# Decode attention with a gated feed-forward on one core: order of the last weight loads, a two-strip result, and x on another queue

## The chip, the core and the metric

The kernel runs on one core of a Trainium2 chip. A core has five engines that run side by side and wait for each other through semaphores: TensorE (PE, matrix products, into PSUM), VectorE (DVE), ScalarE (ACT), GpSimd (POOL) and SyncE (SP, which here only issues transfers). Transfers run on 16 DMA engines; each engine's instruction stream can issue them on a queue of its own. The metric is the time of one execution on the device in microseconds, lower is better.

## What is computed

One decode step of a block with attention and a gated feed-forward in parallel, for batch B = 4, one token, width D = 640:

```python
x = A_x                                   # (4, 1, 640)
xn = layernorm(x)
q = (xn @ wq)                             # 32 heads of 192
k, v = last 2048 rows of the caches       # W = max(256, 8192 // 4)
p = softmax(q k^T * 192**-0.5)
attn = (p v) @ wo                         # (32*192) x 640
ffn = (silu(xn @ w1) * (xn @ w3)) @ w2    # 640 -> 1536 -> 640
return x + attn + ffn                     # bf16
```

All inputs are bf16. Keys and values of 32 heads, four sequences and 2048 rows are 201 MB, and nearly all of the traffic.

## The kernel before, in words

**Tiling.** A head's keys for all four sequences are one tile `kt` of 128 partitions (32 groups of rows by 4 sequences) by 64 rows by 192 elements, 3072 KB; its values are a tile `vt` of the same size. Each is one transfer (`load_k` L97, `load_v` L102). Three buffers each for keys and values. The scores are made on VectorE: per chunk of 16 rows a product with the broadcast q (`mult`, L205), summed in parts by TensorE with an identity (`adder`, L215) and finished by VectorE (`reduce_tile`, L224). Per head follows the softmax (`chain_lmax` to `chain_bc`, exponentials on ScalarE at L256, `rowsum`), then the product with the values on TensorE (`pv`, L275, 32 matmuls into `o_ps`), a copy by ScalarE (L279), and `fold` (L288, L292). Four heads make a group: `ge_tr` (L298 to L300) transposes the group's outputs to `oT` (128 x 6 x 4), and `ge_proj` (L309) multiplies them with the group's output weights into `acc`, two strips of 4 rows by 320 columns at partitions 0 and 32, accumulated over all eight groups.

**Order.** The program order is written out as slots: head h has the four slots 4h to 4h+3, and `add(slot, phase, fn, ...)` puts a piece of work in a slot. The slots end at 128 (`end`), with `pv` nine slots (`L`) behind `mult`. All transfers are issued by SyncE in this order and wait there for their buffer. At the end the order of issues is: key tile 31 and the output weights of the last group (slot 116), value tiles 29 (slot 117), 30 (slot 121) and 31 (slot 125), w1 and w3 (slot 126), and w2 in three parts (slot 128). w1, w3 and w2 take the three key buffers.

**Feed-forward.** `ffn_mm(1)` (slot 138) makes the gate: 15 matmuls into `gt` (L329), a copy (L333) and Silu (L336) on ScalarE, the latter with a load of its function table ahead of it. `ffn_mm(3)` (slot 139) makes the up part with 15 matmuls, a copy (L333) and the product on VectorE (L340). `ffn_transpose` (L346, L347) turns the product into `hT` (128 x 4 x 96). Then 24 matmuls (L406) with w2 give `ff`, again two strips of 4 rows.

**Result.** `acc` is copied strip by strip side by side into a 4 x 640 tile (L397), x is added (L399), the two strips of `ff` are copied by ScalarE (L409) and VectorE (L410), the two are added (L412), and SyncE issues one transfer of the result (L413).

**Start.** SyncE issues x (L113), three transfers of wq into the value buffers (L120) and three key tiles (L99). GpSimd makes the identities and fills the three z tiles (L137). VectorE and ScalarE make the layernorm (L143 to L160), TensorE the q products (L187).

Of the kernel before, what the change touches and what calls it, by code (L numbers as in the profile page):

```python
# [11 lines left out]
BF16 = mybir.dt.bfloat16  # L12
ALU = mybir.AluOpType
# [5 lines left out]
def kernel(  # L19
# [26 lines left out]
    nc = tc.nc  # L46
    P = 128
    B, Sq, D = A_x.shape
    _, H, Sk, Dh = A_k_cache.shape
# [5 lines left out]
    NC = NJ // CH  # L55
# [5 lines left out]
    RPP = (HG * Dh) // P  # L61
# [4 lines left out]
    DH = D // 2  # L66
# [9 lines left out]
    const = ctx.enter_context(tc.tile_pool(name="const", bufs=1))  # L76
# [3 lines left out]
    ppool = ctx.enter_context(tc.tile_pool(name="pr", bufs=PBUFS))  # L80
    qpool = ctx.enter_context(tc.tile_pool(name="qbc", bufs=2))
    opool = ctx.enter_context(tc.tile_pool(name="o", bufs=2))
    small = ctx.enter_context(tc.tile_pool(name="small", bufs=3))
# [3 lines left out]
    ps_acc = ctx.enter_context(tc.tile_pool(name="ps_acc", bufs=1, space=MemoryType.PSUM))  # L87

    kts, vts, prs, pss, scs, zts = {}, {}, {}, {}, {}, {}
    qbcs, wos, o_pss, rss, rcps, o_sbs, o_bfs, ges, chs = ({} for _ in range(9))  # L90
    mult_insts = {}
    ORDER_DEP = mybir.DependencyInfo(mybir.DependencyClass.NoSync, mybir.DependencyReason.SCHED_ONLY)

# [16 lines left out]
        wos[hg] = wt  # L110

    x_sb = const.tile([B, D], BF16, name="x_sb")
    nc.sync.dma_start(out=x_sb[:], in_=A_x.rearrange("b s d -> (b s) d"))  # L113
    RV = NJ * Dh // (H * Dh)
    wq_rows = A_wq.rearrange("(p kc) n -> p kc n", kc=KC)
    wqs = []
# [18 lines left out]
    for i in range(NZ):  # L135
        z = const.tile([P, NJ // 2, 32], BF16, name=f"z{i}")
        nc.gpsimd.memset(z[:], 0.0)  # L137
        zs.append(z)
    rowsel = const.tile([P, 2 * B], FP32, name="rowsel")
    nc.vector.tensor_reduce(out=rowsel[:], in_=idf[:].rearrange("p (g c) -> p c g", g=NG)[:, 0:2 * B, :], axis=AX.X, op=ALU.add)  # L140

# [34 lines left out]
    acc = ps_acc.tile([64, DH], FP32, name="acc")  # L176

    q_pss = []
    for k in range(NB):
        pool, tag = ((ps_add, "ps"), (ps_o, "o_ps"))[k // 2]  # L180
        qp = pool.tile([P, QW], FP32, tag=tag)
        q_pss.append(qp)
    for kc in range(KC):
        for k in range(NB):
            for g in range(NG):
                off = (k * NG + g) * QW
                nc.tensor.matmul(q_pss[k][32 * g:32 * g + 32, :], lhsT=xnT[:, kc, :],  # L187
                                 rhs=wqs[kc // RV][:, kc % RV, off:off + QW], start=(kc == 0), stop=(kc == KC - 1))
# [105 lines left out]
    def ge_tr(hg):  # L294
        gp = ps_t.tile([P, RPP, B], BF16, tag="t")
        of = o_bfs.pop(hg)[:].rearrange("r h d -> r (h d)")
        for i in range(RPP):
            nc.tensor.transpose(out=gp[:, i, :], in_=of[:, i:OW:RPP], identity=idb[0:B, 0:B])  # L298
        oT = small.tile([P, RPP, B], BF16, tag="oT", bufs=2)
        nc.vector.tensor_copy(out=oT[:], in_=gp[:])  # L300
        ges[hg] = oT

    def ge_proj(hg, i):
        oT = ges[hg]
        wo_t = wos[hg]
        st = (hg == 0 and i == 0)
        sp = (hg == H // HG - 1 and i == RPP - 1)
        for t in range(2):
            nc.tensor.matmul(acc[32 * t:32 * t + B, :], lhsT=oT[:, i, :], rhs=wo_t[:, i * D + t * DH:i * D + (t + 1) * DH],  # L309
                             start=st, stop=sp)  # L310

    ffn = {}
# [38 lines left out]
    def add(slot, phase, fn, *args):  # L351
        sched[slot].append((phase, len(sched[slot]), fn, args))

    for h in range(H):
# [4 lines left out]
        for c in range(NC):  # L359
            s = s0 + c  # L360
# [12 lines left out]
        add(max(qg * QP * NC - 3, -1), 6, q_bcast, qg)  # L373
    for hg in range(H // HG):
        a = (hg + 1) * HG * NC - 1 + L
        add(hg * HG * NC + 4, 0, wo_load, hg)
        add(a + 2, 6, ge_tr, hg)
        for i in range(RPP):
            add(a + 3, 6, ge_proj, hg, i)
    hT = const.tile([P, CF, 32 * NF], BF16, name="hT")  # L380

    end = H * NC
    add(end - 2, 0, ffn_load, 1)
    add(end - 2, 0, ffn_load, 3)
    for n in range(NF):
        add(end, 0, w2_load, n)
    add(end + L + 1, 7, ffn_mm, 1)
    add(end + L + 2, 7, ffn_mm, 3)
    add(end + L + 3, 7, ffn_transpose)

    for s in sorted(sched):
        for phase, _, fn, args in sorted(sched[s], key=lambda e: (e[0], e[1])):
            fn(*args)

    attn_bf = ppool.tile([B, D], BF16, tag="pr")
    for t in range(2):
        nc.vector.tensor_copy(out=attn_bf[:, t * DH:(t + 1) * DH], in_=acc[32 * t:32 * t + B, :])  # L397
    t1 = ppool.tile([B, D], BF16, tag="pr")
    nc.vector.tensor_tensor(out=t1[:], in0=x_sb[:], in1=attn_bf[:], op=ALU.add)  # L399

    ff = ps_o.tile([64, DH], FP32, tag="o_ps")
    w2t = ffn[2]
    for n in range(NF):
        for c in range(CF):
            for t in range(2):
                nc.tensor.matmul(ff[32 * t:32 * t + B, :], lhsT=hT[:, c, 32 * n:32 * n + B], rhs=w2t[:, n, c, t * DH:(t + 1) * DH],  # L406
                                 start=(n == 0 and c == 0), stop=(n == NF - 1 and c == CF - 1))
    ffn_bf = ppool.tile([B, D], BF16, tag="pr")
    nc.scalar.copy(out=ffn_bf[:, 0:DH], in_=ff[0:B, :])  # L409
    nc.vector.tensor_copy(out=ffn_bf[:, DH:D], in_=ff[32:32 + B, :])  # L410
    res = ppool.tile([B, D], BF16, tag="pr")
    nc.vector.tensor_tensor(out=res[:], in0=t1[:], in1=ffn_bf[:], op=ALU.add)  # L412
    nc.sync.dma_start(out=out.rearrange("b s d -> (b s) d"), in_=res[:])  # L413


# [28 lines left out]
```

## Time and profile before

| what | value |
|---|---|
| median of 3 runs | 530.42 us (529.5 to 531.95) |
| profiled execution, its own time | 530.08 us |
| profiled execution, span from first to last instruction | 528.3 us |
| HBM read | 222.96 MB, 422 GB/s over the span |
| busy share of TensorE, VectorE, ScalarE, GpSimd | 68%, 64%, 15%, 1% |
| mean granted TensorE clock | 0.848 |
| value tile of head 30, issue to landing | 468.12 us, 34.2 us |
| value tile of head 31, issue to landing | 483.36 us, 26.31 us |
| w1, issue to landing | 483.95 us, 30.3 us |
| w3, issue to landing | 485.1 us, 33.7 us |
| w2 in three parts, first issue; to landing | 494.47 us; 25.8 to 27.0 us |
| table load for Silu | 1.28 us |

The span is what the profile sees of an execution; its own time is 1.78 us longer. A landing is the moment at which the last bytes of a transfer are there. In the profile a line such as `L329 PE MATMUL gt<-wt,xnT` names the source line, the engine, the operation, and the written and read tiles; the granted clock is a share of the full clock of TensorE. In the chain of waits each row is a start, a duration and what the end was waiting for then.

### The profile page before, as it was taken

To read this page: it belongs to the slowest core of one execution; us is meant where nothing else is said; L and a number is where in the kernel's file an instruction comes from. 1 tells how busy PE (TensorE), PEld (TensorE's weight loads), DVE (VectorE), ACT (ScalarE), POOL (GpSimd) and SP (SyncE) were. 2 spreads that over 40 slices of the span, in tenths; PEclk is the share of its full clock that TensorE was granted. 3 is DMA by queue.
4 is the path that set the end of the run, shared out by engine and by line. 5 is a ranking of instruction groups with operands and counts; after the bars stand their busy time and mean duration, and the time that the engine had idled before them with its cause. 6 is when DMAs were issued, how large, how long until landed. Compare 5 with 4: busy or idle time off the path is not lost.

```text
span 528.3 us, 5868 instructions
## 1 busy us (share of the span) xinstructions
PE 360.4 (68%) x2384; PEld 149.5 (28%) x2384; DVE 340.3 (64%) x477; ACT 76.8 (15%) x319; POOL 3.8 (1%) x11
## 2 busy tenths in 40 slices
PE   1456767877577777777566976767587775667765
PEld 1122222332222322223222322223232322223323
DVE  4069766677666657776566677766567776666702
ACT  2101111101111111011111110111111011111112
POOL 2000000000000000000000000000000000000000
PEclk9999988788777887878888787888878878788858
DMA  8999999999999999999999999999999999999994
GB/s 350 424 437 430 432 432 435 427 425 439 432 431 430 429 437 430 434 433 432 428 434 430 429 432 432 430 435 432 426 437 426 433 433 430 431 432 431 432 423 176
DMA packets 11562, 223.33 MB, mean 423 GB/s; under 512 B 1288, under 2 KB 1296, under 8 KB 2704
## 3 DMA queue, kind: packets, MB, share of 16 engines
q1 hardware_dynamic: 11536, 222.97, 98.4%
q8 instruction: 18, 0.29, 0.2%
q14 instruction: 8, 0.07, 0.0%
HBM read 222.96 MB, written 0.01 MB: 422 GB/s over the span
## 4 chain that ended last, share of the span: by engine, by line
DMA 59%; DVE 20%; PE 16%; ACT 3%; issue 1%; SPq 0%; DVEq 0%; ACTq 0%
DMA kt<-in_A_k_cache_dram 54%; DVE pr L205 14%; PE ps L215 10%; DMA vt<-in_A_v_cache_dram 5%; DVE sc L224 4%; PE o_ps L275 3%; ACT z L256 2%; PE acc L309 1%; ACT o_sb L279 1%; PE gt L329 0%; PE gp L298 0%; PE ff L406 0%; PE fp L288 0%; DVE lmax L231 0%; PE tb L262 0%
## 5 line engine op out<-in xcount | busy, mean ns | idle before, releaser
L215 PE MATMUL ps<-pr,idb 128*128 128x512 bf16 x768 | 239.5, 468 | 111.8 <-DVE sc L224 103.3
L205 DVE TENSOR_TENSOR pr<-kt,qbc 128x3072 bf16<-128x3072 bf16 x128 | 223.3, 1746 | 36.7 <-DMA kt<-in_A_k_cache_dram 36.5
L215 PEld LDWEIGHTS <-idb 128*128 128x128 bf16 x768 | 85.1, 114 | 240.3 <-issue 190.6
L224 DVE TENSOR_REDUCE sc<-ps 128x16 f32<-128x512 f32 x128 | 87.0, 680 | 0.6 <-PE ps L215 0.6
L275 PE MATMUL o_ps<-vt,z 128*32 128x384 bf16 x1024 | 56.7, 340 | 3.3 <-DMA vt<-in_A_v_cache_dram 3.3
L256 ACT ACTIVATE z<-sc,negm 128x64 bf16<-128x64 f32 x128 | 45.7, 423 | 89.7 <-DVE negm L252 89.7
L279 ACT COPY o_sb<-o_ps 128x384 f32<-128x384 f32 x32 | 15.1, 472 | 297.9 <-PE o_ps L275 297.9
L252 DVE TENSOR_TENSOR negm<-mt,mbias 128x4 f32<-128x4 f32 x32 | 5.2, 161 | 70.4 <-PE mt L250 70.4
L292 DVE TENSOR_SCALAR o_bf<-fp,rcp 4x192 bf16<-4x192 f32 x32 | 12.9, 405 | 56.1 <-PE fp L288 28.4
L288 PE MATMUL fp<-o_sb,rowsel 128*4 128x192 f32 x128 | 27.3, 338 | 14.6 <-ACT o_sb L279 14.6
L275 PEld LDWEIGHTS <-z 128*32 128x32 bf16 x1024 | 25.7, 98 | 28.5 <-issue 17.5
L256 ACT ACTIVATION_READ_ACCUMULATOR z<-sc,negm 128x1 f32 x128 | 23.9, 187 | 0.0
L288 PEld LDWEIGHTS fp<-o_sb,rowsel 128*4 128x4 f32 x128 | 8.6, 87 | 26.3 <-ACT o_sb L279 21.0
L262 PE MATMUL tb<-ones_f,rs 128*4 128x1 f32 x64 | 6.2, 166 | 12.9 <-ACT z L256 12.9
L250 PE MATMUL mt<-nsc,gmq 1*128 1x4 f32 x64 | 12.2, 258 | 1.3 <-DVE gmq L244 1.3
L250 PEld LDWEIGHTS mt<-nsc,gmq 1*128 1x128 f32 x64 | 9.4, 183 | 12.4 <-issue 10.4
L187 PE MATMUL qp<-wt,xnT 128*32 128x384 bf16 x80 | 7.0, 522 | 6.4 <-DMA wt<-in_A_wq_dram 6.4
L309 PE MATMUL acc<-wt,oT 128*4 128x320 bf16 x96 | 10.6, 307 | 0.6 <-DVE oT L300 0.5
L262 PEld LDWEIGHTS tb<-ones_f,rs 128*4 128x4 f32 x64 | 3.7, 86 | 23.6 <-ACT z L256 22.0
L236 PE MATMUL mt<-idf,lmax 128*1 128x128 f32 x32 | 9.7, 304 | 0.7 <-DVE lmax L231 0.4
L264 DVE RECIPROCAL rcp<-tb 4x1 f32<-4x1 f32 x32 | 4.9, 152 | 8.2 <-PE tb L262 8.2
L199 ACT CAST qbc<-bp 128x384 bf16<-128x384 f32 x16 | 7.6, 485 | 7.7 <-PE bp L196 7.7
(61 smaller groups left out, 81.4 us busy)
## 6 DMA issues: line engine op xcount, KB each, us to landing
kt<-in_A_k_cache_dram SPq DMA_DIRECT2D x32, 3072.0 KB, 36.6
vt<-in_A_v_cache_dram SPq DMA_DIRECT2D x32, 3072.0 KB, 40.3
wt<-in_A_wo_dram SPq DMA_DIRECT2D x8, 960.0 KB, 36.6
wt<-in_A_wq_dram SPq DMA_DIRECT2D x2, 3072.0 KB, 17.0
wt<-in_B_w_dram SPq DMA_DIRECT2D x2, 1920.0 KB, 32.0
w2t<-in_B_w_dram SPq DMA_DIRECT2D x3, 640.0 KB, 26.4
wt<-in_A_wq_dram SPq DMA_DIRECT2D x1, 1536.0 KB, 20.2
x_sb<-in_A_x_dram SPq DMA_DIRECT2D x1, 5.0 KB
```

The lines of the kernel that those rows point to most:

```text
L205: mi = nc.vector.tensor_tensor(out=pr[:], in0=kts[h][:, c * CH:(c + 1) * CH, :], in1=qbcs[h // QP][:, h % QP, :].unsqueeze(1).to_broadcast ...
L215: nc.tensor.matmul(ps[:], lhsT=idb[:], rhs=pr[:, :, kk * DD:(kk + 1) * DD], start=(kk == 0), stop=(kk == NK - 1))
L224: ri = nc.vector.tensor_reduce(out=scs[h][:, c * CH:(c + 1) * CH], in_=pss.pop(s)[:], axis=AX.X, op=ALU.add)
L236: nc.tensor.transpose(out=mt[0:1, 0:P], in_=chs[h][0][:], identity=idf[:])
L250: nc.tensor.matmul(mt[:, P:P + B], lhsT=gmq[:].rearrange("o q b -> o (q b)"), rhs=nsc[:], start=True, stop=True)
L256: nc.scalar.activation(out=z[:, :, 0:2, b], in_=sc[:].rearrange("p (j s) -> p j s", s=2), func=ACTF.Exp, bias=negm[:, b:b + 1], scale=SCAL ...
L262: nc.tensor.matmul(tb[:], lhsT=rss.pop(h)[:], rhs=ones_f[:], start=True, stop=True)
L275: nc.tensor.matmul(o_ps[32 * g:32 * g + 32, :], lhsT=z[:, jj, :], rhs=vt[:, 2 * jj:2 * jj + 2, :], start=(jj < NG), stop=(jj >= NJ // 2 - NG))
L279: nc.scalar.copy(out=o_sb[:].rearrange("r two d -> r (two d)"), in_=o_pss.pop(h)[:])
L288: nc.tensor.matmul(fp[:], lhsT=rowsel[:, two * B:(two + 1) * B], rhs=o_sb[:, two, :], start=(two == 0), stop=(two == 1))
L292: nc.vector.tensor_scalar_mul(out=o_bfs[hg][:, hl, :], in0=fp[:], scalar1=rcps.pop(h)[:, 0:1])
L309: nc.tensor.matmul(acc[32 * t:32 * t + B, :], lhsT=oT[:, i, :], rhs=wo_t[:, i * D + t * DH:i * D + (t + 1) * DH], start=st, stop=sp)
```

## The change

Five edits:

- **Loads.** w1 is issued in slot 124, ahead of value tile 31 (slot 125); the output weights of the last group move from slot 116 to slot 126, behind that tile; w3 goes to slot 127; w2 stays in slot 128.
- **Gate.** `ffn_mm(1)` moves from slot 138 to slot 133, phase 0, which is ahead of the value matmuls of head 31; `ffn_mm(3)` takes slot 138. On TensorE the order is then: value matmuls of head 30, gate, fold of head 30, value matmuls and fold of head 31, transposes, projection, up, transposes, w2. On ScalarE the gate's copy, the table load and Silu stand ahead of head 31's copy.
- **32-column weights.** `oT` becomes two fixed tiles of 32 columns per step, filled with zeros once by GpSimd, of which 4 columns are written per group; the projection and the w2 matmuls use 32 columns, so that all 64 rows of `acc` and `ff` are written.
- **Result.** The two strips stay where they are: one copy of `acc` (64 x 320), one add of `x_st`, and one add that reads `ff` from PSUM; two transfers of the result, one on SyncE's queue and one on ScalarE's.
- **x.** x is loaded on ScalarE's queue, followed there by two small transfers into the two strips of `x_st`, which GpSimd fills with zeros first.

```diff
-    nc.sync.dma_start(out=x_sb[:], in_=A_x.rearrange("b s d -> (b s) d"))
+    x_rows = A_x.rearrange("b s d -> (b s) d")
+    nc.scalar.dma_start(out=x_sb[:], in_=x_rows)
+    x_st = const.tile([64, DH], BF16, name="x_st")
+    nc.gpsimd.memset(x_st[:], 0.0)
+    for t in range(2):
+        nc.scalar.dma_start(out=x_st[32 * t:32 * t + B, :], in_=x_rows[:, t * DH:(t + 1) * DH])
...
+    oTs = []
+    for i in range(2):
+        oT = const.tile([P, RPP, 32], BF16, name=f"oT{i}")
+        nc.gpsimd.memset(oT[:], 0.0)
+        oTs.append(oT)
...
-        oT = small.tile([P, RPP, B], BF16, tag="oT", bufs=2)
-        nc.vector.tensor_copy(out=oT[:], in_=gp[:])
-        ges[hg] = oT
+        nc.vector.tensor_copy(out=oTs[hg % 2][:, :, 0:B], in_=gp[:])
...
-            nc.tensor.matmul(acc[32 * t:32 * t + B, :], lhsT=oT[:, i, :], rhs=wo_t[:, i * D + t * DH:i * D + (t + 1) * DH],
+            nc.tensor.matmul(acc[32 * t:32 * t + 32, :], lhsT=oT[:, i, :], rhs=wo_t[:, i * D + t * DH:i * D + (t + 1) * DH],
                              start=st, stop=sp)
...
-        add(hg * HG * NC + 4, 0, wo_load, hg)
+        add(hg * HG * NC + (4 if hg < H // HG - 1 else 14), 0, wo_load, hg)
...
     end = H * NC
-    add(end - 2, 0, ffn_load, 1)
-    add(end - 2, 0, ffn_load, 3)
+    add(end - 4, 0, ffn_load, 1)
+    add(end - 1, 0, ffn_load, 3)
     for n in range(NF):
         add(end, 0, w2_load, n)
-    add(end + L + 1, 7, ffn_mm, 1)
-    add(end + L + 2, 7, ffn_mm, 3)
+    add(end + L - NC, 0, ffn_mm, 1)
+    add(end + L + 1, 7, ffn_mm, 3)
     add(end + L + 3, 7, ffn_transpose)
...
-    attn_bf = ppool.tile([B, D], BF16, tag="pr")
-    for t in range(2):
-        nc.vector.tensor_copy(out=attn_bf[:, t * DH:(t + 1) * DH], in_=acc[32 * t:32 * t + B, :])
-    t1 = ppool.tile([B, D], BF16, tag="pr")
-    nc.vector.tensor_tensor(out=t1[:], in0=x_sb[:], in1=attn_bf[:], op=ALU.add)
+    attn_bf = ppool.tile([64, DH], BF16, tag="pr")
+    nc.vector.tensor_copy(out=attn_bf[:], in_=acc[:])
+    t1 = ppool.tile([64, DH], BF16, tag="pr")
+    nc.vector.tensor_tensor(out=t1[:], in0=x_st[:], in1=attn_bf[:], op=ALU.add)
...
-                nc.tensor.matmul(ff[32 * t:32 * t + B, :], lhsT=hT[:, c, 32 * n:32 * n + B], rhs=w2t[:, n, c, t * DH:(t + 1) * DH],
+                nc.tensor.matmul(ff[32 * t:32 * t + 32, :], lhsT=hT[:, c, 32 * n:32 * n + 32], rhs=w2t[:, n, c, t * DH:(t + 1) * DH],
                                  start=(n == 0 and c == 0), stop=(n == NF - 1 and c == CF - 1))
-    ffn_bf = ppool.tile([B, D], BF16, tag="pr")
-    nc.scalar.copy(out=ffn_bf[:, 0:DH], in_=ff[0:B, :])
-    nc.vector.tensor_copy(out=ffn_bf[:, DH:D], in_=ff[32:32 + B, :])
-    res = ppool.tile([B, D], BF16, tag="pr")
-    nc.vector.tensor_tensor(out=res[:], in0=t1[:], in1=ffn_bf[:], op=ALU.add)
-    nc.sync.dma_start(out=out.rearrange("b s d -> (b s) d"), in_=res[:])
+    res = ppool.tile([64, DH], BF16, tag="pr")
+    nc.vector.tensor_tensor(out=res[:], in0=ff[:], in1=t1[:], op=ALU.add)
+    out_rows = out.rearrange("b s d -> (b s) d")
+    nc.sync.dma_start(out=out_rows[:, 0:DH], in_=res[0:B])
+    nc.scalar.dma_start(out=out_rows[:, DH:D], in_=res[32:32 + B])
```

More of the change, by code (lines that the diff above doesn't have):

```diff
@@ L89 @@
     kts, vts, prs, pss, scs, zts = {}, {}, {}, {}, {}, {}
-    qbcs, wos, o_pss, rss, rcps, o_sbs, o_bfs, ges, chs = ({} for _ in range(9))
+    qbcs, wos, o_pss, rss, rcps, o_sbs, o_bfs, chs = ({} for _ in range(8))
     mult_insts = {}
@@ L298, in ge_tr @@
             nc.tensor.transpose(out=gp[:, i, :], in_=of[:, i:OW:RPP], identity=idb[0:B, 0:B])
-        oT = small.tile([P, RPP, B], BF16, tag="oT", bufs=2)
-        nc.vector.tensor_copy(out=oT[:], in_=gp[:])
-        ges[hg] = oT
+        nc.vector.tensor_copy(out=oTs[hg % 2][:, :, 0:B], in_=gp[:])
     def ge_proj(hg, i):
-        oT = ges[hg]
+        oT = oTs[hg % 2]
         wo_t = wos[hg]
```

## The prediction

> **What bounds the kernel now.** I read the page first (span, slices, queue rows), then the chain of waits over the last 20 us, then the timeline and the issue rows of the end and of the start, then the stretches in which the granted TensorE clock changed. The slices show one resource that is full:
>
> ```profile
> span 528.3 us, 5868 instructions
> ...
> PEclk9999988788777887878888787888878878788858
> DMA  8999999999999999999999999999999999999994
> ...
> q1 hardware_dynamic: 11536, 222.97, 98.4%
> ```
>
> The transfer engines are busy from the first slice to the last; no other engine is. So the time is three pieces: what passes before the stream starts, the stream of 223 MB, and what follows its last bytes. The change moves no byte out of the stream, so it can touch only the ends. The end, in the chain of waits:
>
> ```profile
> 483.36 26.31 DMA vt<-in_A_v_cache_dram
> ...
> 516.44 2.27 PE gt L329 x10
> 518.72 0.02 issue
> 518.74 0.58 ACT t_bf L333
> 519.32 0.02 issue
> 519.34 1.28 ACT L336
> 520.62 0.01 issue
> 520.63 0.63 ACT sg L336
> 521.26 0.48 ACT t_bf L333
> ...
> 523.05 1.84 PE ff L406 x24
> 524.89 0.02 issue
> 524.91 0.49 DVE ffn_bf L410
> ...
> 525.50 0.48 DVE res L412
> ```
>
> The last value tile (head 31) lands at 483.36 + 26.31 = 509.67. Behind it come the attention output, the gate matmuls, then on ScalarE copy, table load (1.28 us), Silu and a second copy, one after the other; then product, transposes, 24 output matmuls, copy, add. The result is ready at 525.98, and 2.32 us later the span ends. Beside that chain the stream itself runs on: w3, issued at 485.1, takes 33.7 us and lands at 518.8, and by the stretches of 0.15 us the last w2 packets move until about 522.9. The chain starts its w2 matmuls at 523.05, so the two are only 0.1 us apart there.
>
> **The change, part by part.**
>
> *Order of transfers.* w1 (1920 KB) goes ahead of the head-31 value tile, and the last output-weight group (960 KB) from ahead of it to behind it; the sum up to w3 stays. A 3072 KB value tile took 7.31 us (502.36 to 509.67), so 960 KB is 2.28 us and 1920 KB 4.57 us. Head 30's value tile lands at 500.08 instead of 502.36, w1 at 504.65 (before about 514.25), head 31's at 511.95, 2.28 us later than before; the output weights at 514.2; w3 and w2 where they were. SyncE's waits don't starve the stream: w1 takes the buffer of key tile 29, whose products ended before 465, so it issues right behind value tile 30 (468.1); value tile 31 still issues near 483.4, w3 behind it, w2 at 494.5, each over 23 us ahead of its landing.
>
> *Gate matmuls.* They now stand on TensorE ahead of head 31's value matmuls; behind the wait for w1 stand the fold of head 30 and then head 31, and nobody needs those before 511.5. Cover: 504.65 to 511.95. At half clock the gate takes 2.5 us (13 took 2.45 us there), then copy 0.58, table 1.28, Silu 0.63, all over by 510. This takes 1.28 + 0.63 us of ScalarE out of the end; what is late next is w3, at 518.8. Head 31's own chain (2.75 value matmuls, 0.60 copy, 1.46 fold, 0.48, 0.47, 0.23, then 12 projection matmuls, about 1.7 at half clock) ends at 519.6 at half clock and near 516.9 at full clock, so w3 is the later one wherever the clock is full.
>
> *x on ScalarE's queue.* The first wq issue moves from 1.15 to 0.73, as x's issue (0.35 us, start 0.73) leaves SyncE: 0.42 us for the whole stream, if first bytes follow issue. Bounds: 0 (if the engines weren't ready) to 0.42; I take 0.42, because the issue rows are back to back and wq's bytes start within 0.9 us of the issue. What x now shares with wq: even 4 us late it is hidden, since the first product waited for the first key tile at 30.41 while q was ready at 25.24. ScalarE's three issues (about 1.1 us) and the wait for the small fill on GpSimd stand ahead of the table load, and that is used first at 6.28. The third key tile's issue waits for x's landing; 1.5 us of wait against some 18 us of wq queued. Cost nothing. GpSimd's three new fills (at most 0.9 us each, as the z fills) lie behind z, used after 45, and the identity is late by some 0.2 us of slack.
>
> *32 columns instead of 4.* The same matmul count and moved columns; the weight loads of 32 columns took 98 ns (z) and those of 4 columns 86 or 87 ns, and overlap. From -0.1 to +0.3 us over 24 matmuls; I take 0.
>
> *The result.* Out: copy 0.49 + add 0.48 with gaps, 524.89 to 525.98 = 1.09 us. In: one add of 64x320 from PSUM; nearest rows are the 4x320 cast from PSUM (0.49) and the 4x640 add (0.48): bounds 0.3 to 0.6, I take 0.49 + 0.03. One copy and the add with x lie under the transposes and the w2 matmuls, as their two copies did. Two output transfers of 2.5 KB on two queues replace one of 5 KB: 2.32 us from result to end, bounds 2.1 to 2.7; I keep 2.32.
>
> *Sum*, all 0.42 earlier: w3 518.38; up matmuls 1.36 at full clock (row at 518.82) 519.74; copy 0.60 520.34; product 0.46 520.80; transposes 0.42 521.22; copy 0.40 521.62; 24 w2 matmuls 1.88 523.50 (the last eight start at 522.9, the stream ends at 522.5: no wait); add 0.52 524.02. Before: 525.98. Gain 1.96 us (0.42 start, 0.57 result, the rest the ScalarE chain): 530.08 - 1.96 = **528.1 us**, against the median of 530.42 it is 2.3 us or 0.44%.
>
> **The clock, which could undo it.** The granted clock changes at 491.09, 501.33 and 518.39, all multiples of 3.41 us apart:
>
> ```profile
> 497.92:501.33 3.41, 1.61 (x21) 0.73 (x9) 0.88 (x4) 1.32 (x7) 0.00 (x0) 1.00 0.94 404
> 501.33:504.74 3.41, 2.54 (x34) 1.43 (x33) 0.16 (x1) 1.44 (x8) 0.00 (x0) 0.50 1.02 440
> ...
> 511.57:514.98 3.41, 2.34 (x16) 0.51 (x8) 0.40 (x1) 0.48 (x1) 0.00 (x0) 0.50 1.00 426
> 514.98:518.39 3.41, 3.08 (x27) 2.12 (x29) 0.18 (x2) 0.00 (x0) 0.00 (x0) 0.50 0.97 407
> 518.39:521.81 3.42, 1.78 (x25) 1.08 (x20) 0.05 (x1) 2.96 (x4) 0.00 (x0) 1.00 0.62 258
> ```
>
> The third column is TensorE's busy time, the third from the end its clock. 1.61 us busy in 3.41 lost the full clock; 2.54 did not win it back, 3.08 did (2.63 did at 351.14). Before, the long run of projection, gate and up matmuls brought it back; the change takes the gate out of that run. On this grid the sum goes: value tile 30 and gate fill 501.33 to 504.74 with about 2.8 us (clock up), 508.16 to 511.57 is empty (down), 511.57 to 514.98 holds 2.75 us of head 31 (up), 514.98 to 518.39 holds about 2.1 us, more than the 1.61 that lost it (stays). So the up and w2 matmuls run at full clock, as summed. Where the grid lies against the kernel is chance; head 31 has 4.2 us of work in 4.8, which holds a whole stretch for about half of the positions.
>
> [...]
>
> **The rivals.**
>
> *The last transfer sets the end* (faster by a little more). If the up chain is 0.6 us shorter than summed, the last eight matmuls wait for w2: 522.5 + 0.66 + 0.52 + 2.32 = 526.0 of span, 527.8; with a quicker small output 527.6. For: the two are 1 us apart. Against: six steps would each have to be shorter.
>
> *The clock returns late*, inside the up matmuls: 1.36 becomes up to 2.5, 529.2. For: the other half of the grid positions. Against: this execution's own grid.
>
> *The clock doesn't return* (slower). TensorE's half rate, from head 31 to the end: 511.53 + 7.7 = 519.2 for the projection, up matmuls 2.5, then 0.61, 0.46, 0.55, 0.40, w2 matmuls 2 x 1.8, add 0.52: result 527.9, 1.9 later than before, 532.0. It decides from the point at which no 3.41 us stretch between 511.5 and 519 holds 2.6 us of work. For: the gate is gone from the run, and 2.54 us were not enough. Against: 2.75 + 1.44 us stand close together.
>
> *The change doesn't do what it says*: the transfers land in issue order now (value tile 509.67, w1 514.25, w3 518.8), so the new order takes hold; no chance of its own.
>
> **How the numbers follow.** Forecast 0.56, transfer-bound 0.20, late clock 0.15, no clock 0.09. I call 0.5% (2.65 us) about what a measurement can tell, so faster means under 527.8: half of the forecast's cases (it lies 0.3 above the bound, and the median shown lies 0.34 above the profiled execution) and all of the transfer-bound ones, 0.48. Slower (over 533.1) takes the no-clock case with the upper part of the spread of the runs shown (1.5 above the median): 0.05. The rest is 0.47. The range: from 527.6 less 1.2 (the lowest run is 0.9 under the median, and the output's 0.3), 526.4, to 529.2 plus the 1.5, 530.8, which leaves the no-clock case out.
>
> **What would show it.** Right: SyncE's first wq issue near 0.7; in the chain of waits the up matmuls wait for w3 near 518.4 and the table load near 507 is off the chain; head 31's value matmuls near 511.5 to 512; the add ends about 2.3 us before the span. Wrong: w2 matmuls of 3 us or more (clock), w2 matmuls that wait for w2 (transfer), a DMA slice that is not full (a wait of SyncE), or a stream that starts no earlier.

## The result, and the profile after

The changed kernel takes 532.57 us (median of 10 runs, 531.41 to 534.6); the kernel before takes 530.06 us (median of 10 runs beside them, 529.38 to 531.95). The ratio is 1.0046, with a 95% interval from 1.0031 to 1.0062: slower by about 2.4 us, where 528.1 and a gain were forecast. The profiled execution took 532.7 us.

The page of the changed kernel, its span and its main transfer queue:

```profile
span 530.9 us, 5871 instructions
...
q1 hardware_dynamic: 11528, 222.96, 98.3%
...
HBM read 222.96 MB, written 0.01 MB: 420 GB/s over the span
```

The same bytes, and the transfer engines as busy, but 420 instead of 422 GB/s over a longer span. The chain of waits over the last 25 us shows the end (start, duration, what the end was waiting for):

```profile
487.51 33.88 DMA wt<-in_B_w_dram
521.39 0.04 issue
521.44 1.28 PE gt L337 x15
...
522.74 0.59 ACT t_bf L341
...
523.35 0.43 DVE hb L348
...
524.64 3.25 PE ff L413 x24
...
527.92 0.48 DVE res L416
```

The edits did what they say. The table load and Silu have left the chain, the up matmuls are released by w3, the result takes one add of 0.48 us where a copy and an add took 1.09. But two numbers are far from the forecast. w3 lands at 521.39, not at 518.38. And the 24 w2 matmuls take 3.25 us, not 1.88.

The first is not made at the end. One long stretch in the middle of the run, 40 to 480 us, where neither kernel does anything new (busy time and instructions of PE, PEld, DVE, ACT and POOL, the granted clock, the share of the transfer engines, GB/s); first the kernel before, then the changed one:

```profile
40.00:480.00 440.00, 314.22 (x2008) 128.26 (x2011) 307.88 (x422) 61.32 (x275) 0.00 (x0) 0.84 1.01 432
```

```profile
40.00:480.00 440.00, 315.82 (x1984) 128.81 (x1983) 305.50 (x418) 61.35 (x275) 0.00 (x0) 0.82 1.00 429
```

The transfer engines are full in both, yet they move 432 and 429 GB/s. 3 in 430 over some 500 us is about 3.5 us, as far as rounded rates can tell: the stream itself has become slower, all the way through, and w3 lands 2.6 us later than the 518.8 of before.

What differs there? One thing that the prediction did not look at is where the tiles lie in SBUF. The constants come first, then the key buffers, then the value buffers. The change adds to the constants one `x_st` of 320 x 2 = 640 bytes per partition and two `oT` of 6 x 32 x 2 = 384 bytes (the old `oT` lay behind the buffers), 1408 bytes in all. The key buffers start at byte 30720 of each partition before, a multiple of 512, and at 32128 now, 384 bytes over one; the value buffers, a multiple of 24576 behind, are shifted alike. The row that a transfer writes into one partition is 24576 bytes long.

The start did what was forecast at first, but kept little of it. The timeline of the changed kernel:

```profile
0.73 1.42 SPq L125 DMA_DIRECT2D wt<-in_A_wq_dram  x3
...
30.36 5.09 DVE L215 TENSOR_TENSOR pr<-kt,qbc 128x3072 bf16<-128x3072 bf16 x3 [19.09 <-DMA kt<-in_A_k_cache_dram]
```

The first wq issue is at 0.73 instead of 1.15, but VectorE's first product, which waits for the first key tile, starts at 30.36 instead of 30.41: 0.42 us ahead, 0.05 us ahead 30 us later. In the executions of the kernel before and of its variants with the old start, shown further down, the same product starts anywhere from 30.23 to 30.67, so that one execution can't tell a gain or loss of 0.05 us. VectorE's product itself takes as long as before (mean 1745 ns, 1746 before), so reading the shifted tiles costs nothing there.

### The profile page after: what moved, and what is told of

It reads as the page before. It is cut to its first block, busy times and chain, and to the rows that moved or that the text cites. A ratio compares the mean times of both kernels' runs of the same rounds, so it can differ in the third digit from the quotient of the medians.

```text
span 530.9 us, 5871 instructions
## 1 busy us (share of the span) xinstructions
PE 363.6 (68%) x2384; PEld 149.9 (28%) x2384; DVE 339.8 (64%) x475; ACT 76.4 (14%) x318; POOL 4.5 (1%) x14
## 4 chain that ended last, share of the span: by engine, by line
DMA 61%; DVE 22%; PE 12%; ACT 3%; issue 2%; SPq 0%; DVEq 0%; ACTq 0%
DMA kt<-in_A_k_cache_dram 54%; DVE pr L215 16%; PE ps L225 7%; DMA wt<-in_B_w_dram 6%; DVE sc L234 5%; PE o_ps L285 2%; ACT z L266 2%; PE acc L317 1%; ACT o_sb L289 1%; PE ff L413 1%; DVE lmax L241 0%; PE tb L272 0%; SPq L125 0%; PE gt L337 0%; SPq L109 0%
## 5 line engine op out<-in xcount | busy, mean ns | idle before, releaser
L225 PE MATMUL ps<-pr,idb 128*128 128x512 bf16 x768 | 243.5, 474 | 110.3 <-DVE sc L234 101.5
L215 DVE TENSOR_TENSOR pr<-kt,qbc 128x3072 bf16<-128x3072 bf16 x128 | 223.2, 1745 | 37.8 <-DMA kt<-in_A_k_cache_dram 37.6
L225 PEld LDWEIGHTS <-idb 128*128 128x128 bf16 x768 | 86.4, 116 | 241.6 <-issue 193.7
L285 PE MATMUL o_ps<-vt,z 128*32 128x384 bf16 x1024 | 55.6, 334 | 3.8 <-DMA vt<-in_A_v_cache_dram 3.8
L317 PE MATMUL acc<-wt,oT 128*32 128x320 bf16 x96 | 10.0, 301 | 0.7 <-DVE oT L309 0.5
```

Source lines behind the costliest of these rows:

```text
L215: mi = nc.vector.tensor_tensor(out=pr[:], in0=kts[h][:, c * CH:(c + 1) * CH, :], in1=qbcs[h // QP][:, h % QP, :].unsqueeze(1).to_broadcast ...
L225: nc.tensor.matmul(ps[:], lhsT=idb[:], rhs=pr[:, :, kk * DD:(kk + 1) * DD], start=(kk == 0), stop=(kk == NK - 1))
L285: nc.tensor.matmul(o_ps[32 * g:32 * g + 32, :], lhsT=z[:, jj, :], rhs=vt[:, 2 * jj:2 * jj + 2, :], start=(jj < NG), stop=(jj >= NJ // 2 - NG))
L317: nc.tensor.matmul(acc[32 * t:32 * t + 32, :], lhsT=oT[:, i, :], rhs=wo_t[:, i * D + t * DH:i * D + (t + 1) * DH], start=st, stop=sp)
```

## The experiments

Three theories at first: the *placement* of the tiles makes the transfers slower; a second active *queue* (x on ScalarE's) does; the new *order* of the loads does. Beside them stands the clock of the last matmuls, which can explain only the 1.4 us at the very end. Each run's ratio is against the kernel before, timed on the same chip in the same rounds.

### Placement put back, in the changed kernel

```diff
+    pad = const.tile([P, 64], BF16, name="pad")
+    nc.gpsimd.memset(pad[:], 0.0)
     rowsel = const.tile([P, 2 * B], FP32, name="rowsel")
```

> The changed kernel with one unused constant tile of 128 bytes per partition more, so that the key and value tiles start at a multiple of 512 bytes of SBUF again (before: 30720; changed: 32128, which is 384 over a multiple of 512). Placement theory: the steady transfer rate comes back from about 429 to 432 GB/s, w3 lands near 518.4 instead of 521.4, the time is 528 to 529.6, 0.1 to 0.4% under before. Queue theory (x and half of the result on ScalarE's queue slow the stream): nothing changes, 532.5, rate 429. Order theory (the moved loads cost the time): 532.5 as well. If it were only the clock of the last 24 matmuls (3.25 us instead of 1.84), w3 would still land near 521.4.

Measured: 529.02 us (12 runs), ratio 0.9986 (0.9972 to 0.9999). 128 unused bytes per partition make the changed kernel over 3 us faster (0.60% between the two ratios) and turn its loss into a small gain. The same stretch, and the chain of waits over the end:

```profile
40.00:480.00 440.00, 316.81 (x2006) 129.13 (x2008) 307.87 (x422) 61.35 (x275) 0.00 (x0) 0.84 1.00 431
```

```profile
495.38 27.77 DMA w2t<-in_B_w_dram
523.14 0.04 issue
523.18 0.73 PE ff L415 x8
523.92 0.02 issue
523.94 0.48 DVE res L418
```

The rate is back at 431 (432 was expected), and what ends last is now a transfer: the last part of w2 lands at 523.14, eight matmuls and the add follow.

### The same shift in the kernel before

```diff
+    pad = const.tile([P, 192], BF16, name="pad")
+    nc.gpsimd.memset(pad[:], 0.0)
     rowsel = const.tile([P, 2 * B], FP32, name="rowsel")
```

> The kernel before with one unused constant tile of 384 bytes per partition, so that its key and value tiles start 384 bytes over a multiple of 512, as in the changed kernel; nothing else differs. Placement theory: the rate falls from 432 to 429 GB/s, the time is 532.5 to 533.5, 0.5 to 0.65% over before. Queue and order theories: same as before, 530.

Measured: 533.15 us (6 runs), ratio 1.0051 (1.0036 to 1.0067), and in the same stretch

```profile
40.00:480.00 440.00, 314.59 (x1983) 128.01 (x1983) 305.38 (x418) 61.35 (x275) 0.00 (x0) 0.83 1.01 430
```

Nothing but unused bytes was added, and the kernel before loses 2.7 us. So placement alone can produce the loss; the queue and order theories said no change here. The traces' records of single transfer packets show where: the 8448 packets of 24576 bytes, a row each, take 914.6 ns on average in the kernel before, 99% of them 912 ns at most, and 917.8 ns here, 917.9 in the changed kernel, 914.5 with the placement put back. That is 0.35% longer; the rest of the 0.51% isn't seen in them. The unused bytes also shift the constants and work tiles behind them; the runs don't move the streamed tiles quite alone.

### x back on SyncE's queue

```diff
-    nc.scalar.dma_start(out=x_sb[:], in_=x_rows)
+    nc.sync.dma_start(out=x_sb[:], in_=x_rows)
...
-        nc.scalar.dma_start(out=x_st[32 * t:32 * t + B, :], in_=x_rows[:, t * DH:(t + 1) * DH])
+        nc.sync.dma_start(out=x_st[32 * t:32 * t + B, :], in_=x_rows[:, t * DH:(t + 1) * DH])
```

> The changed kernel with x and its two strips loaded by SyncE, ahead of wq, as x was before. Queue theory: the rate returns to 432 GB/s and the time to 529 to 530 (the start is about 1.5 us later by three issues and the wait for the fill). Placement theory: the rate stays at 429 and the time is 533 to 534.5, the changed kernel plus the later start.

Measured: 533.36 us (6 runs), ratio 1.0054 (1.0038 to 1.0069). The loss stays, and with it the rate of 429 GB/s between 40 and 480 us, so the second queue isn't its cause. The first product starts at 31.15 here against 30.36 in the changed kernel, which is the later start.

### The order of loads and the gate alone

The kernel before with the edits of the loads and of `ffn_mm`, as in the change, and nothing else.

> The kernel before with the moved loads and the moved gate alone (w1 ahead of the last value tile, the last output weights behind it, the gate ahead of the last value matmuls); x, the result and the 4-column weights as before, tiles at a multiple of 512 bytes. Placement theory: rate 432, w3 lands at 518.8; the end gains up to 1.0 us where the clock is full and loses up to 1.0 us where the w2 matmuls run at half clock: 529 to 531, unresolved against 530.06. Order theory: 532.5, with w3 near 521.4.

Measured: 529.92 us (12 runs), ratio 0.9997 (0.9983 to 1.001). The order costs nothing (the rate is 431 GB/s). Nor does it bring a gain that this comparison resolves, and the chain of waits of its profiled execution shows a part of the reason:

```profile
495.49 27.85 DMA w2t<-in_B_w_dram
523.34 0.04 issue
523.38 0.75 PE ff L406 x8
524.13 0.02 issue
524.15 0.49 DVE ffn_bf L410
```

Head 31's value matmuls start at 512.00 and the up matmuls at 518.84 (forecast for the order without the start: 511.95 and 518.8), the w2 matmuls at 522.04 instead of 523.05. That is the 1 us that leaves the chain. But now the last eight matmuls wait for the last part of w2, until 523.34, which gives back some 0.25 us: the 24 matmuls end 2.09 us after their start, where 1.84 were needed without a wait.

The larger part is that this 1 us depends on the clock. The old order, with 256 unused bytes (next section) and the gate at full clock in its profiled execution (13 of its matmuls took 1.38 us, 2.45 in the profile before), already has it. Rows of that execution:

```profile
515.70 1.38 PE L331 MATMUL gt<-wt,xnT 128*32 128x512 bf16 x13
...
518.86 1.26 PE L331 MATMUL gt<-wt,xnT 128*32 128x512 bf16 x15 [1.38 <-DMA wt<-in_B_w_dram]
...
522.07 2.10 PE L408 MATMUL ff<-w2t,hT 128*4 128x320 bf16 x24 [0.45 <-DVE hT L349]
```

There the table load runs from 517.73 and Silu ends at 519.65, under the up matmuls that wait for w3; the w2 matmuls start at 522.07, as with the new order. So in these executions the order takes something off the end only where the gate would run at half clock.

### Which boundary it is

The kernel before with 256 and with 64 unused bytes (`[P, 128]` and `[P, 32]` in the edit above).

> The kernel before with 256 bytes of unused constant, so that the key and value tiles start 256 over a multiple of 512. If the rule is a multiple of 256 bytes: 530.2 and 432 GB/s, as before. If it is a multiple of 512: 533, as with 384 bytes.

Measured: 530.27 us (12 runs), ratio 0.9997 (0.9988 to 1.0007): the tiles may start 256 bytes over a multiple of 512.

> The kernel before with 64 bytes of unused constant (the tiles start 64 over a multiple of 512). If each row that starts off the boundary costs one more write whatever the offset is: 533, as with 384. If the cost grows with the offset: between 530.2 and 533. If a multiple of 64 is enough: 530.2.

Measured: 533.54 us (5 runs), ratio 1.0051 (1.0038 to 1.0063). The same stretch with 256 bytes and with 64 bytes:

```profile
40.00:480.00 440.00, 315.20 (x2021) 129.15 (x2023) 308.27 (x423) 61.34 (x275) 0.00 (x0) 0.83 1.01 431
```

```profile
40.00:480.00 440.00, 311.38 (x1983) 126.74 (x1982) 305.50 (x419) 61.35 (x275) 0.00 (x0) 0.83 1.00 429
```

64 bytes and 384 bytes (128 over a multiple of 256) cost the same 0.51%, 256 bytes cost nothing. The mean time of a row's packet says the same: 918.3 ns with 64 bytes, 914.5 with 256. So what counts, in these offsets, is whether the rows start on a boundary of 256 bytes, and not by how much they miss it. What a row off the boundary does more, one more write as the expectation supposes or something else, no run shows.

### One half off the boundary

64 bytes ahead of the key buffers, and 192 between them and the value buffers, so that only the keys and w1, w3, w2 miss the boundary; then the complement, 64 bytes between the two.

```diff
     kpool = ctx.enter_context(tc.tile_pool(name="kt", bufs=KBUFS))
+    gpool = ctx.enter_context(tc.tile_pool(name="gap", bufs=1))
     vpool = ctx.enter_context(tc.tile_pool(name="vt", bufs=VBUFS))
...
+    pad = const.tile([P, 32], BF16, name="pad")
+    nc.gpsimd.memset(pad[:], 0.0)
+    gap = gpool.tile([P, 96], BF16, name="gap")
+    nc.gpsimd.memset(gap[:], 0.0)
```

> The kernel before with 64 bytes of constant ahead of the key buffers and 192 bytes between them and the value buffers: the key tiles and the three feed-forward weights in their buffers start 64 bytes over a boundary of 256, the value tiles, wq and the output weights start on one. 104 of some 218 MB, 48%, then lands off the boundary. If the cost is paid per row that lands off it: 0.48 of the 2.7 us, 531.6 to 531.9, a ratio near 1.0025. If one off-boundary buffer set slows the whole stream: 533, 1.005. If only the value buffers matter: 530.3, 1.000.

Measured: 530.94 us (12 runs), ratio 1.0009 (0.9998 to 1.002). Less than the 1.0025 that a cost per row would give, and not the 1.005 of a cost to the whole stream either. With the interval of the whole loss (0.38 to 0.63%) a cost per row could be as low as 1.0018, which this interval still holds.

> The complement: the kernel before with 64 bytes between the key and the value buffers, so that the key tiles and w1, w3 and w2 start on a boundary of 256 bytes and the value tiles, wq and the output weights 64 over it (52% of the bytes). With the keys off, the ratio was 1.0009 (0.9998 to 1.002) and w3 landed by 519.7, 0.9 later than before. Cost per row: 0.52 of 2.7 us, a ratio of 1.0026, w3 near 520.2. If the value buffers carry the rest: 1.004, w3 near 520.7. If any mixture costs little and only all buffers off cost much: 1.001.

Measured: 531.17 us (12 runs), ratio 1.0016 (1.0007 to 1.0026): a cost per row holds, at the edge of the interval, and so does the 1.001 of a mixture that costs little; the 1.004 that the other half would need to make up the rest doesn't. The two halves add up to 0.25%, against 0.51% with everything off. The time from VectorE's first product to the start of head 31's value matmuls tells the same more sharply, since the different starts drop out of it. One execution each:

| the kernel before with | first product | head 31 | between | more than before |
|---|---|---|---|---|
| nothing added | 30.41 | 509.72 | 479.31 | |
| 256 bytes | 30.53 | 509.78 | 479.25 | -0.06 |
| keys off by 64 | 30.47 | 510.47 | 480.00 | 0.69 |
| values off by 64 | 30.67 | 510.92 | 480.25 | 0.94 |
| all off by 384 | 30.23 | 512.20 | 481.97 | 2.66 |
| all off by 64 | 30.44 | 512.35 | 481.91 | 2.60 |

0.69 and 0.94 make 1.63, not 2.6, where the two kernels on the boundary differ by 0.06 and the two with everything off by 0.06. The packet records agree: 92% of the rows' packets still take 912 ns at most with the keys off and 75% with the values off, but 10% and 27% with everything off by 64 and by 384. So in these executions the loss isn't a fixed cost per row off the boundary: with half of the rows off it costs less than half. The reason stays open.

### x on ScalarE's queue alone

```diff
-    nc.sync.dma_start(out=x_sb[:], in_=A_x.rearrange("b s d -> (b s) d"))
+    nc.scalar.dma_start(out=x_sb[:], in_=A_x.rearrange("b s d -> (b s) d"))
```

> The kernel before with x on ScalarE's queue and nothing else. If the whole 0.42 us of the earlier first issue reaches the stream, w3 lands at 518.4 instead of 518.8 and the time is 0.4 less, 529.8; if the start gives it back, w3 lands at 518.8 and the time is the same.

Measured: 529.35 us (10 runs), ratio 0.9983 (0.9974 to 0.9992), a gain of 0.9 us (0.4 to 1.4). The up matmuls, released by w3, start at 518.61 in its profiled execution; they started at 518.82 before, right behind the gate. Of the 0.42 us some 0.2 can be seen at w3; the ratio leaves room for all of it. But the 0.9 us can't be put down to the start alone. In this execution the gate ran at full clock (13 matmuls in 1.38 us) and the w2 matmuls start at 521.82, 1.2 us earlier than in the profile before, most of which is the clock; how many of the ten runs had it isn't known. The second queue costs the stream nothing that the rate shows: it is 431 GB/s. Here, too, the constants keep their size.

### The clock at the end

The changed kernel with its tiles on the boundary fell into two groups of runs: seven from 528.37 to 529.10, four from 529.84 to 529.97 (and one of 532.01). To test whether the clock of the w2 matmuls splits them, 11 matmuls were put into TensorE's gaps behind head 31's value matmuls (2), the fold (2), the projection (2), the up matmuls (4) and the transposes (1).

```diff
+            fi = nc.tensor.matmul(fill["t"][:], lhsT=idb[:], rhs=q_sb[:, 0, :], start=True, stop=True)
+            tc.add_manual_dep(fi.ins, last[key].ins.name, ORDER_DEP, reason="filler behind it")
...
-    add(end + L + 1, 7, ffn_mm, 3)
+    add(end + L - 1, 7, filler, 2, "pv")
+    add(end + L, 7, filler, 2, "fold")
+    add(end + L + 2, 7, filler, 2, "proj")
+    add(end + L + 2, 8, ffn_mm, 3)
+    add(end + L + 2, 9, filler, 4, "gate")
     add(end + L + 3, 7, ffn_transpose)
+    add(end + L + 3, 8, filler, 1, "tr")
```

> The changed kernel with its tiles at a multiple of 512, and 11 filler matmuls (128x384, into a PSUM tile that nobody reads) in the gaps of TensorE behind head 31's value matmuls, fold, projection, up matmuls and transposes. Its runs without fillers fell into two groups, around 528.7 and around 529.9. Clock theory: the upper group is the one in which the w2 matmuls run at half clock; with fillers it goes away, the median is 528.5 to 528.8 and the w2 matmuls end 0.73 us behind the last transfer. Rival (the two groups come from the transfers): two groups as before, median 529.0, or the fillers delay the up matmuls by up to 0.6 us and it gets slower.

Measured: 529.16 us (9 runs, 528.77 to 529.72), ratio 0.9978 (0.9968 to 0.9987). Neither theory came out clean: the spread is narrower (0.95 us against 1.6 without the outlier) and no run lies above 529.72, but the median isn't lower than without fillers, and the two ratios' intervals overlap. In its profiled execution the last part of w2 lands at 523.28 and the eight matmuls take 0.73 us, as expected at full clock; but they did so without fillers too, in a run of the lower group, so this doesn't show what the upper group is. That the clock splits the groups is not shown. By its ratio it is the fastest of all kernels run here; against the changed kernel with 128 bytes the comparison doesn't decide.

## Why the prediction was wrong

**The step that failed** is the sentence on which the sum stood: "The change moves no byte out of the stream, so it can touch only the ends." The change moved where the bytes land. 1408 bytes of constants put every streamed row 128 bytes over a boundary of 256, and the stream lost 0.5% of its rate over its whole length. The same shift alone costs the kernel before 0.51%; taking it back alone brings the changed kernel from a ratio of 1.0046 to 0.9986. The two together, 0.51% less 0.14%, give 0.37%, inside the measured 0.31 to 0.62%. The added constants were in the prediction, but only as fills on GpSimd, costed at nothing. In the profiled execution the sum closes: the result is ready at 528.40 where 524.02 was forecast, 3.01 us of it because w3 lands late, 1.37 because the w2 matmuls take 3.25 us and not 1.88.

**The order of transfers** was right: 511.95 and 518.8 were forecast without the start, 512.00 and 518.84 measured in the run with the order alone. ScalarE's copy, table load and Silu left the chain, as forecast. **What that is worth** was mis-sized: the sum took it, 0.97 us, from one execution in which the gate ran at half clock, and where the gate runs at full clock the old order has it already. The run with the order alone measured 0.9997 (0.9983 to 1.001).

**What takes their place** was mis-sized too. The forecast let the w2 matmuls run without a wait, with the stream ending at 522.5. With the tiles on the boundary the last part of w2 lands at 523.14, 523.28 and 523.34 in three executions, and the last eight matmuls wait for it. That wait is the one in the rival "The last transfer sets the end", but not as told there: the chain isn't shorter than summed, the landing is later, and the wait makes nothing faster. I had read the end of the stream off the stretches in which packets still move (522.9) and taken the whole 0.42 us of the start from it. Where the landing is 523.14, the last packets move until 522.7 in the same trace: 0.2 us of the start arrived, and the landing that releases TensorE came 0.4 us behind the packets.

So the profiled execution with the tiles on the boundary has its result at 524.42, 0.4 us behind the 524.02 of the sum: 0.2 from the start and 0.2 from that wait. It took 528.72 us, 1.36 less than the profiled execution before. Over all runs the gain is only about 0.7 (ratio 0.9986; by its interval between nothing and 1.5), while this execution is one of the lower group of its kernel and the one before ran its gate at half clock; what the clock gave or took in each run isn't resolved.

**x on ScalarE's queue** was right in its sign: w3 lands some 0.2 us earlier of the 0.42 taken. The 0.17% of that edit alone holds an unknown share of clock. x arrived at 2.23 instead of 2.20, and the layernorm behind it stays hidden under the wait for the first key tile (19.09 us of idle VectorE ahead of it). **The result** was right in its add: one of 0.48 us in place of 1.09 us. From the result to the end of the span it takes 2.5 us with two transfers, in the changed kernel and in the one on the boundary, where 2.32 was kept, inside the bounds given. The matmuls with 32 columns took no longer: eight of the 24 took 0.73 us with 32 columns, 0.75 with 4.

**The clock** was named, and its return came as forecast, but the forecast picked the wrong case for this execution. The stretches of the changed kernel between its clock changes (columns as in the stretches of the prediction):

```profile
513.92:517.34 3.42, 2.75 (x32) 1.21 (x31) 0.00 (x0) 0.04 (x1) 0.00 (x0) 0.50 1.02 428
517.34:520.75 3.41, 2.16 (x22) 1.23 (x23) 0.57 (x2) 0.44 (x1) 0.00 (x0) 1.00 0.96 396
520.75:524.16 3.41, 1.67 (x21) 0.69 (x18) 0.81 (x2) 0.58 (x1) 0.00 (x0) 1.00 0.57 234
524.16:527.58 3.42, 2.97 (x25) 1.65 (x24) 0.59 (x3) 0.00 (x0) 0.00 (x0) 0.50 0.05 21
```

Head 31's 2.75 us of value matmuls brought the clock up, as forecast. The up matmuls and the transposes then filled only 1.67 us of their stretch, and the clock fell at 524.16, 0.5 us before the w2 matmuls started: 3.25 us instead of about 1.84, 1.4 us in this execution. The grid lay elsewhere in this one: an edge at 517.34 where the profile before has one at 518.39, 1.05 us apart on a grid of 3.41. A case in which the clock comes back and is lost again before the w2 matmuls was not among those listed. Nor was the test "more than the 1.61 that lost it" safe: in the profile before, the clock was also lost behind a stretch with 2.33 us (361.38 to 364.79) and kept behind one with 1.67 (436.47 to 439.89). Since the end waits for w2 when the tiles are on the boundary, how much of these 1.4 us a median holds wasn't resolved; the fillers only narrowed the spread.

**The slower side** held 0.05, for a clock that stays down throughout. The kernel became slower by another way, which none of the rivals named.

## What to carry to other kernels

Where a kernel is bound by its transfers, the start address of the tiles that they fill is part of the change: add up the bytes that an edit puts ahead of them in each partition, and pad so that long rows start on a multiple of 256 bytes; rows of 24576 bytes that started 64 or 128 bytes over one cost 0.51% here, rows that started on one cost nothing (0.9997). When the full resource moves fewer bytes per microsecond at the same busy share (429 instead of 432 GB/s at 1.00 and 1.01 here), look at a stretch in the middle of the run before explaining the end. And of a chain that is shortened at the end, ask when the last transfer has landed, not when its packets thin out (0.4 us earlier here), and ask whether the chain is as long in other executions: here about half of the forecast gain, 0.97 of 1.96 us, came from the clock of one execution.

## What the runs showed of the hardware that was not expected

- Transfers of 24576-byte rows into SBUF lose 0.51% (1.0038 to 1.0063, and 1.0036 to 1.0067) when the rows start 64 or 128 bytes over a boundary of 256, and nothing (0.9988 to 1.0007) when they start on one that is no multiple of 512. The share of time for which the transfer engines count as busy doesn't show it (1.00 and 1.01); the rate does, and the mean time of a row's packet (917.8 to 918.3 ns off the boundary, 914.5 to 914.6 on it).
- With only the keys or only the values off the boundary the stretch to head 31 is 0.69 and 0.94 us longer, with both 2.6: the parts don't add up to the whole.
- The landing that released TensorE (523.14) came 0.4 us behind the last packets of the trace (522.7).
- TensorE's clock was lost at the end of stretches of 3.41 us with 1.61 us of work (before) and 1.67 us (after), but also with 2.33 us, and kept with 1.67 (both before): the work in one stretch alone doesn't tell.
